# Weights of 40 columns instead of 64 in the state increments of an mLSTM and mixture kernel

## The chip, the cores and the metric

The kernel runs on one core of a Trainium2 chip. The metric is the device time of one execution in microseconds. Three runs of the kernel before took 291.7, 292.54 and 294.46 us; the median is 292.54 us.

## The reference

The first half is an mLSTM attention over 4 batches, 8 heads, 768 steps and a head size of 40. Per step it keeps a matrix state, a vector state and a running maximum of the gates:

```python
m_new = np.maximum(f_gate[:, :, t] + m, i_gate[:, :, t])
f_stab = np.exp(f_gate[:, :, t] + m - m_new)
i_stab = np.exp(i_gate[:, :, t] - m_new)
C = f_stab[:, :, None, None] * C + i_stab[:, :, None, None] * np.einsum('bhd,bhe->bhde', vt, kt)
n = f_stab[:, :, None] * n + i_stab[:, :, None] * kt
y[:, :, t] = o * (C q) / max(|n q|, 1)
```

The second half takes the 320 values per step and runs four experts of causal softmax attention (width 64). Each step's two experts are chosen and weighted by a small gate, and their outputs are projected and summed.

## The kernel before, in words

**Chunks.** The recurrence is worked in chunks of 128 steps, 6 per batch, 24 in all, and each chunk has two subchunks of 64. Inside a chunk the contribution of earlier steps is a masked product (`p1_intra`). What comes from before a subchunk is the state: a table per head of 40 rows (the key's dimensions) by 41 columns (40 value columns and one of ones, which carries the vector state). `p1_inc` forms the state's increment of each subchunk, `sums` adds the masked part and the carried part, and `p1_state` divides by the denominator and applies the output gate.

**Who takes which path.** Chunks 0 to 3 (`NARROW = 4`) go through `inc_narrow`, with weights of 128 rows and 40 columns, and aren't touched. The other 20 go through `p1_inc` (line 1078). Sixteen of them compute both subchunks; the last chunk of each batch computes one.

**The layout.** Even and odd heads lie in the two halves of the partitions for `ks` (the keys times their decay) and `nat` (values and keys). Per head `ks` has `T` = 64 columns; the 40 data columns are rewritten for each chunk by GpSimd, and columns 40 to 63 are zeroed once at the start (line 1551). One increment matmul takes 64 rows of `ks` as weights and 41 columns of `nat` as the moving side, and writes a 64-row half of a bank, so four of them fit on the array side by side. With `wide` (true for every chunk, line 1086), all 64 columns are the weights, so that rows 40 to 63 of the result come out as zeros.

**The evacuation.** Two tiles `pdc` hold the increments. For each subchunk GpSimd multiplies the old state by its decay (`cd`, 112 rows), and VectorE adds the increment to it and writes a tile `sts`. The rows taken are 0 to 111 (`GR` = 64 + 48). The product that uses the state (`carried`, line 1124) reads rows 0 to 39 and 64 to 103, called `heads`.

**The order.** Every engine's instructions are first recorded, and then a planner (`plan`, line 361) puts them in order with prices of its own. It looks up to twelve groups ahead on TensorE where it models a stall of over 350 ns, gives copies to one of two engines by their due times, and times the transfers of SyncE by due times too. The price of a matmul is in `matmul_time` (line 340); for 32-bit weights it is

```python
t = n * 4 / 2.27 + 3
t = max(t, 1.7 * lhs.free_size())
```

with `n` the moving columns and `lhs.free_size()` the weight columns. Due times add these prices up. All instructions are issued from one helper, so the profile gives them all line 618, and tiles tell them apart: `one` is the ring of eight banks of PSUM.

Of the kernel before, what the change touches and what calls it, by code (L numbers as in the profile page):

```python
# [14 lines left out]
B, H, S, D = 4, 8, 768, 40  # L15
# [3 lines left out]
NCH = S // P  # L19
HALF = S // 2  # L20
D1 = D + 1
T = P // 2
RP = 48
GR = T + RP
# [611 lines left out]
def mlstm_moe_kernel(ctx, tc, kq, nat, ig, fg, wqkv, wo, const, out):  # L636
# [9 lines left out]
    def buf(tag, shape, dtype=F32):  # L646
        return View(Buf(rings[tag], shape, dtype))
# [17 lines left out]
    def one(name):  # L665
        tape.cut()
        return buf("one", [P, 512])

    rows = slice(0, T), slice(T, P)
    heads = slice(0, D), slice(T, T + D)  # L670
# [49 lines left out]
    def first(b, j):  # L720
        return b == 0 and j < 3
# [4 lines left out]
    def narrow(b, j):  # L726

        return b * NCH + j < NARROW
# [349 lines left out]
    def p1_inc(b, j):  # L1078
        if narrow(b, j):
            return inc_narrow(b, j)  # L1080
        nm = f"{b}_{j}"
        nt, qc, dm, ks = p1st.pop((b, j, "c"))
        n0 = (b * NCH + j) * 2
        sprev = state[b] if j else None
        sin = [sprev]
        wide = b * NCH + j < 24
        subs = range(2 if j < NCH - 1 else 1)
        pdc = [one(f"pdc_{nm}_{a}") for a in range(2)]
        tape.cut(True)
        for sub in subs:  # L1090
            for g in range(2):
                for z in range(2):
                    for r, p in zip(rows, pdc):
                        nc.tensor.matmul(
                            p[(rows if wide else heads)[z], (2 * sub + g) * D1 : (2 * sub + g + 1) * D1],
                            ks[r, sub, 2 * z + g, 0 : T if wide else D],
                            nt[r, (sub * 4 + 2 * z + g) * D1 : (sub * 4 + 2 * z + g + 1) * D1],
                            start=True,
                            stop=True,
                        )  # L1100
        tape.cut()
        for sub in subs:
            cn = sts[(n0 + sub + 1) % len(sts)][:, : 4 * D1].rearrange("p (g d) -> p g d", g=4)
            if sprev:
                cd = buf("cd", [GR, 4, D1], F32)
                (tape.either if first(b, j) else nc.gpsimd.tensor_tensor)(
                    cd,
                    sprev,
                    dec[:, :, b, 2 * j + sub : 2 * j + sub + 1].to_broadcast([GR, 4, D1]),
                    op=ALU.mult,  # L1110
                )
            for a in range(2):
                x = pdc[a][:, 2 * sub * D1 : 2 * (sub + 1) * D1].rearrange("p (g d) -> p g d", g=2)
                for r in (slice(0, GR),) if wide else heads:
                    if sprev:
                        nc.vector.tensor_tensor(cn[r, a::2, :], x[r], cd[r, a::2, :], op=ALU.add)
                    else:
                        nc.vector.tensor_copy(cn[r, a::2, :], x[r])
            sprev = cn
            sin.append(cn)  # L1120
        state[b] = sprev
        p1st[(b, j, "i")] = (nt, qc, dm, sin)
# [451 lines left out]
    spread(0, 1)  # L1574
    p1_prep(0, 1)
    p1_inc(0, 0)
    p1_intra(0, 1)
    p1_state(0, 0)
    spread(0, 2)
    p1_prep(0, 2)  # L1580
    p1_inc(0, 1)
    p1_intra(0, 2)
    p1_state(0, 1)
    p1_out(0, 0)
    p1_inc(0, 2)
    p1_state(0, 2)
    p1_out(0, 1)
# [110 lines left out]
    for f in LAST.split():  # L1698
        g = dict(f=flip, r=factors, s=score, m=mix, p=project, q=h["queries"], k=h["keys"], v=h["values"], g=h["gate"])
# [65 lines left out]
```

## Time and profile before

| | |
|---|---|
| median of 3 runs | 292.54 us (291.7 to 294.46) |
| profiled execution, span | 291.4 us (the page lists no time of its own beside the span) |
| TensorE matmuls | 279.5 us busy, 96% |
| TensorE weight loads | 242.2 us, 83% |
| VectorE | 220.7 us, 76% |
| ScalarE | 213.8 us, 73% |
| GpSimd | 166.5 us, 57% |
| mean granted clock of TensorE | 0.993 |

A busy time is the sum of the stretches in which at least one instruction of the engine runs. Matmuls overlap, on up to four tiles of the array, and their ends are modelled, so a busy TensorE isn't one at its peak. Weight loads have a row of their own and run beside the matmuls.

### The profile page before, as it was taken

What the parts mean: (1) busy time and instruction counts of PE and PEld (TensorE: products, weight loads), DVE (VectorE), ACT (ScalarE), POOL (GpSimd) and SP (SyncE); (2) the same over time, 40 slices, a digit from 0 to 9 for tenths busy, and PEclk for the clock granted to TensorE, in tenths of its full rate; (3) what the DMA queues carried; (4) which work ended last, traced back from release to release, by engine and by line L of the source; (5) the groups of instructions that cost most, each with busy time, mean ns of one, the idle gap of its engine ahead of it and who ended that gap; (6) DMA issues with size and microseconds to landing.
All of it is one profiled execution on the core that took longest, in us unless ns stands there. A gap on an engine that the chain in (4) does not pass through costs nothing.

```text
span 291.4 us, 12993 instructions
## 1 busy us (share of the span) xinstructions
PE 279.5 (96%) x5128; PEld 242.2 (83%) x5128; DVE 220.7 (76%) x852; ACT 213.8 (73%) x714; POOL 166.5 (57%) x284
## 2 busy tenths in 40 slices
PE   8988999869999999999999999999999999999994
PEld 3876898759889978799889978798989976987884
DVE  7679387847896897657886888577878895588983
ACT  8983459829895887657895887567876895597971
POOL 3678298858889556958587628955870341014000
PEclk9999999979999999999999999999999999999999
DMA  7989769983566455645453537625401000100101
GB/s 217 293 262 282 188 178 236 251 188 110 130 194 184 116 157 167 172 124 169 137 173 112 170 100 200 196 95 146 133 6 71 2 0 2 71 3 0 70 26 45
DMA packets 31580, 39.18 MB, mean 134 GB/s; under 512 B 2784, under 2 KB 25280, under 8 KB 31520
## 3 DMA queue, kind: packets, MB, share of 16 engines
q1 hardware_dynamic: 31472, 38.26, 45.9%
q8 instruction: 40, 0.66, 0.9%
q14 instruction: 20, 0.16, 0.2%
q10 hardware_dynamic: 48, 0.10, 0.1%
HBM read 34.22 MB, written 4.13 MB: 132 GB/s over the span
## 4 chain that ended last, share of the span: by engine, by line
PE 74%; DVE 8%; ACT 5%; issue 4%; DMA 4%; POOL 3%; SPq 1%; DVEq 0%; ACTq 0%; POOLq 0%
PE one L618 74%; DMA nat<-in_nat 4%; ACT dm L618 2%; DVE A L618 2%; POOL qs L618 1%; SPq L618 1%; DVE one L618 1%; DVE sts L618 1%; ACT A L618 1%; POOL yl L618 1%; ACT AT L618 1%; DVE dm L618 0%; DVE facb L618 0%; POOL xt L618 0%; DVE xt L618 0%
## 5 line engine op out<-in xcount | busy, mean ns | idle before, releaser
L618 ACT ACTIVATE A<-A,nmx 128x128 f32<-128x128 f32 (+5 forms) x96 | 64.0, 671 | 3.7 <-DVE nmx L618 3.5
L618 DVE CUSTOM_DVE_ANT_0 A<-one,maskw 128x384 f32<-128x384 f32 (+4 forms) x96 | 45.0, 495 | 0.4
L618 ACT ACTIVATE AT<-one 128x256 f32<-128x256 f32 (+3 forms) x96 | 35.5, 428 | 6.3 <-PE one L618 6.1
L618 PE MATMUL one<-AT,V 128*64 128x384 f32 (+2 forms) x360 | 39.8, 370 | 0.0
L618 PE MATMUL one<-xl,WH 128*128 128x384 f32 x96 | 33.2, 346 | 2.3 <-issue 2.3
L618 PE MATMUL one<-xh,WH 128*128 128x384 f32 x96 | 34.7, 361 | 0.5 <-DVE xt L618 0.5
L618 PEld LDWEIGHTS one<-AT,V 128*64 128x64 f32 x360 | 22.5, 137 | 14.9 <-issue 11.6
L618 POOL TENSOR_TENSOR qs<-kqs,eqs 112x512 f32<-112x512 f32 x20 | 26.2, 1311 | 10.8 <-PE one L618 10.5
L618 PE MATMUL one<-cst,A 64*128 64x64 f32 x672 | 31.6, 226 | 0.0
L618 PEld LDWEIGHTS one<-cst,A 64*128 64x128 f32 x672 | 27.5, 138 | 2.9 <-issue 0.6
L618 POOL TENSOR_TENSOR dm<-dm,cst 128x512 f32<-128x512 f32 x20 | 25.7, 1286 | 6.3 <-DMA dm<-gd 5.0
L618 PE MATMUL one<-KH,QH 64*128 64x384 f32 (+4 forms) x128 | 27.2, 375 | 0.0
L618 POOL TENSOR_TENSOR ks<-nat,dm 128x320 f32<-128x320 f32 x24 | 17.8, 743 | 14.5 <-ACT dm L618 6.9
L618 PE MATMUL one<-KL,QH 64*128 64x384 f32 (+4 forms) x128 | 23.9, 319 | 0.0
L618 PE MATMUL one<-KH,QL 64*128 64x384 f32 (+4 forms) x128 | 23.8, 319 | 0.0
L618 DVE COPY AT<-one 128x384 f32<-128x384 f32 (+3 forms) x48 | 21.0, 456 | 2.5 <-PE one L618 2.2
L618 PEld LDWEIGHTS one<-xh,WH 128*128 128x128 f32 x96 | 18.5, 193 | 4.6 <-issue 3.4
L618 ACT ACTIVATE xh<-one 128x192 fp32r<-128x192 f32 (+1 forms) x45 | 13.0, 335 | 12.3 <-PE one L618 12.2
L618 PE MATMUL one<-xh,WL 128*128 128x384 f32 x64 | 22.0, 343 | 0.0
L618 PE MATMUL one<-WH,xh 128*128 128x260 f32 x72 | 21.5, 301 | 0.0
L618 DVE TENSOR_TENSOR dm<-one,dm 128x256 f32<-128x256 f32 (+1 forms) x44 | 18.7, 440 | 3.3 <-POOL ks L618 3.1
L618 DVE CUSTOM_DVE_ANT_0 A<-one,maskw,nmx 128x320 f32<-128x320 f32 (+1 forms) x32 | 18.5, 579 | 2.8 <-DVE nmx L618 1.0
(143 smaller groups left out, 812.9 us busy)
## 6 DMA issues: line engine op xcount, KB each, us to landing
kqs<-in_kq SPq DMA_DIRECT2D x24, 448.0 KB, 5.6
nat<-in_nat SPq DMA_DIRECT2D x20, 484.0 KB, 5.7
dm<-gd SPq DMA_DIRECT2D x40, 128.0 KB, 3.7
eqs<-ge SPq DMA_DIRECT2D x40, 96.0 KB, 5.3
out<-ob SPq DMA_DIRECT2D x24, 160.0 KB, 1.9
nat<-in_nat SPq DMA_DIRECT2D x4, 320.0 KB, 6.4
A<-in_wqkv SPq DMA_DIRECT2D x3, 386.0 KB, 6.8
nat<-in_nat SPq DMA_DIRECT2D x8, 82.0 KB, 6.3
```

The lines of the kernel that those rows point to most:

```text
L618: f(*[fix(x) for x in op.a], **{k: fix(v) for k, v in op.k.items()})
```

## The change

The increments of the 20 chunks load 40 columns of `ks` as weights and write rows 0 to 39 and 64 to 103 of the bank. The evacuation takes rows 0 to 103 in one instruction. Rows 40 to 63 are then whatever the bank held.

```diff
-        wide = b * NCH + j < 24
...
-                            p[(rows if wide else heads)[z], (2 * sub + g) * D1 : (2 * sub + g + 1) * D1],
-                            ks[r, sub, 2 * z + g, 0 : T if wide else D],
+                            p[heads[z], (2 * sub + g) * D1 : (2 * sub + g + 1) * D1],
+                            ks[r, sub, 2 * z + g, 0:D],
                             nt[r, (sub * 4 + 2 * z + g) * D1 : (sub * 4 + 2 * z + g + 1) * D1],
...
-                for r in (slice(0, GR),) if wide else heads:
+                for r in (slice(0, T + D),):
```

## Rows read from the trace of the kernel before

**Rows 1.** The page: engines' busy times, slices of the span, and the instruction queue.

```profile
PE 279.5 (96%) x5128; PEld 242.2 (83%) x5128; DVE 220.7 (76%) x852; ACT 213.8 (73%) x714; POOL 166.5 (57%) x284
...
PEclk9999999979999999999999999999999999999999
DMA  7989769983566455645453537625401000100101
...
q8 instruction: 40, 0.66, 0.9%
```

**Rows 2.** Stretches: length, busy time and count per engine, granted clock, transfer share, GB/s.

```profile
45.90:59.00 13.10, 11.87 (x368) 10.49 (x369) 11.63 (x57) 11.38 (x52) 11.43 (x15) 1.00 0.99 239
59.00:61.40 2.40, 0.10 (x1) 0.00 (x0) 1.81 (x8) 0.35 (x2) 2.24 (x5) 1.00 1.12 224
61.40:66.00 4.60, 4.56 (x27) 4.21 (x27) 0.56 (x1) 1.38 (x3) 1.52 (x5) 0.63 0.54 145
66.00:114.00 48.00, 47.98 (x1036) 42.69 (x1036) 39.35 (x160) 39.55 (x134) 35.36 (x56) 1.00 0.51 143
114.00:226.00 112.00, 111.54 (x2294) 98.76 (x2290) 85.58 (x344) 82.67 (x280) 74.59 (x122) 1.00 0.46 138
```

**Rows 3.** Waits of TensorE: total us, times, longest us.

```profile
PE one L618 <- issue: 2.3, 1, 2.3
PE one L618 <- DVE sts L618: 1.6, 2, 0.9
```

**Rows 4.** Weight loads by form: rows x columns, count, busy us, mean ns.

```profile
L618 PEld LDWEIGHTS one<-nat,ks 64*64 64x64 f32 x576 | 11.6, 134 | 0.6 <-issue 0.2 <-POOL ks L618 0.2
...
L618 PEld LDWEIGHTS one<-nat,ks 128*40 128x40 f32 x64 | 2.5, 115 | 1.7 <-POOL ks L618 1.7
```

**Rows 5.** Timeline of increments: start us, us from first start to last end.

```profile
13.54 0.74 PE L618 MATMUL one<-nat,ks 128*40 128x82 f32 x16
...
131.44 0.63 PE L618 MATMUL one<-nat,ks 64*64 64x41 f32 x32
...
131.38 0.56 PEld L618 LDWEIGHTS one<-nat,ks 64*64 64x64 f32 x32
```

**Rows 6.** The increments' matmuls by form.

```profile
L618 PE MATMUL one<-nat,ks 128*40 128x82 f32 x64 | 3.0, 235 | 1.2 <-POOL ks L618 1.2
```

**Rows 7.** One short stretch, increments alone: busy us and count of matmuls, of loads, of GpSimd.

```profile
131.44:131.53 0.09, 0.09 (x9) 0.09 (x12) 0.00 (x0) 1.00 0.00 0
```

**Rows 8.** Stretches, loads of the increments alone: length, busy us and count.

```profile
43.00:44.50 1.50, 0.56 (x32) 1.00 1.11 242
...
66.00:226.00 160.00, 9.37 (x464) 1.00 0.48 140
```

**Rows 9.** VectorE sums by form: the state's evacuation, and another sum.

```profile
L618 DVE TENSOR_TENSOR sts<-one,cd 112x82 f32<-112x82 f32 x66 | 12.9, 230 | 5.3 <-POOL cd L618 4.0 <-PE one L618 0.9
...
L618 DVE TENSOR_TENSOR one<-one,pc 64x82 f32<-64x82 f32 x6 | 1.3, 258 | 0.6 <-ACT pc L618 0.6
```

**Rows 10.** Timeline of TensorE around the pause at 59 us.

```profile
61.44 0.33 PE L618 MATMUL one<-xl,WH 128*128 128x384 f32 x1 [2.34 <-issue]
...
61.96 0.51 PE L618 MATMUL one<-xl,WH 128*128 128x384 f32 x1
...
65.15 0.44 PE L618 MATMUL one<-xl,WH 128*128 128x384 f32 x1
...
69.35 0.34 PE L618 MATMUL one<-xl,WH 128*128 128x384 f32 x1
69.53 0.34 PE L618 MATMUL one<-xh,WH 128*128 128x384 f32 x1
```

## The prediction

> **What bounds the kernel now.** I read the page's busy times first, then a table of stretches, then the waits of TensorE. The page shows TensorE busy in nearly every slice and every other engine well below it; the transfers are full only at the start [rows 1]. The stretches say where this holds [rows 2]: from 66 us to 226 us TensorE is busy 159.5 of 160 us (47.98 and 111.54), with VectorE at 0.76 to 0.82, ScalarE at 0.74 to 0.82 and GpSimd at 0.67 to 0.74. Before that, from 45.9 to 59, TensorE is idle 1.2 us and the transfer engines are 0.99 busy; from 59 to 61.4 it stands nearly still. The waits agree [rows 3]: one pause of 2.3 us that waits for no instruction, and a few waits under 1 us. So after 66 us a shorter piece of TensorE work should come through to the end; before 61.4 us it should mostly turn into waiting.
>
> **The weight loads.** A 32-bit matmul of the code stands in the trace as two loads and two matmuls, so the 576 loads of 64 x 64 are the 288 matmuls that the change touches [rows 4]. Does the load set their pace? In an undisturbed group, 32 loads take 0.56 us from the first start to the last end [rows 5]. Less one load of 0.134 us, that is 0.43 us over 31 steps, 13.7 ns each; four array tiles take turns, so each tile is loaded anew every 55 ns, one round. The matmul side would allow less: 16 matmuls of 82 columns on two tiles take 0.74 us in the opening stage [rows 5], less one of 0.235 [rows 6] that is 33.7 ns a step and 67 ns a round, or 34 ns for 41 columns. The load therefore sets the round. Its row falls from 134 to 115 ns when it has 40 columns instead of 64 [rows 4], 19 ns less, which leaves 36 ns by weights.
>
> A third limit is how fast TensorE starts instructions. The group's first matmul starts at 131.44 [rows 5], and from there to 131.53 nine of them have begun [rows 7]: 10 ns apart, 40 ns for a round of four. This is the fastest that the trace shows for this form, and it is above both 36 and 34, so I take 40 ns. The saving is 15 ns a round. Its bounds are 0 (the start rate under load is no better than now) and 55 - 34 = 21 ns.
>
> [...]
>
> **How many rounds count.** Of the 576 loads 464 lie between 66 and 226 us [rows 8], where TensorE has no idle time: 116 rounds, 116 x 15 = 1.7 us (0 to 2.4). The other 112 loads, 28 rounds and 0.4 us, lie from 43 to 58 us, the first of their four groups ahead of 44.5 us [rows 8]; TensorE waits there for transfers and for the pause at 59 us, so I put them at 0 and keep 0.4 us for the range.
>
> **The evacuation.** The same VectorE instructions run with the same free size, on 104 partitions instead of 112. A sum of 82 columns takes 230 ns on 112 partitions, and a like one takes 258 ns on 64 [rows 9]: the time does not follow the partitions. I take 0; 8 fewer partitions reach no row that is read later. Rows 40 to 63 now carry what an earlier user left in the bank, but the carried product takes only rows 0 to 39 and 64 to 103. No instruction is added, and the GpSimd product that decays the state still has its shape, so no queue grows and no new wait stands ahead of anything.
>
> **The written order.** The planner prices one of these matmuls at max(41 x 4 / 2.27 + 3, 1.7 x columns): 109 ns with 64 and 75 ns with 40. Its TensorE time shrinks by about 4 x 34 = 0.13 us for each full chunk, so engine choices for copies and the order on every queue can change from the fifth chunk on, and due times a little earlier. No row prices a queue that isn't written yet. As the expected value I take 0, since the groups that TensorE runs stay the same and it looks ahead only past modelled stalls of 350 ns; the bounds come from the rivals.
>
> **The sum.** 291.4 us span, less 1.7, is 289.7 us. The page gives no device time of this execution beyond its span; the runs lie 0.3 to 3.1 us above it, their median 1.1 us. On the median: 292.5 - 1.7 = 290.8 us.
>
> **Rivals.**
>
> *Nothing comes through.* The start rate stays at 13.7 ns, or VectorE, ScalarE and GpSimd set the pace as soon as TensorE gives way. For: at 0.74 to 0.82 they are not far off, and a TensorE that is always busy in the table may still hold hidden waits, since ends are modelled. Against: 464 loads sit where no wait of TensorE is listed. It gives 292.5 us. That the array tile is loaded as 64 columns whatever the slice would give the same; the 115 ns row speaks against it, though it comes from full-height loads.
>
> [...]
>
> [...]
>
> *The rewritten order is worse.* The state's evacuation comes up behind a score evacuation on VectorE, and TensorE waits for it. The longest such wait now is 0.9 us and there are two [rows 3]. In one chunk in three of the sixteen in which the state is carried after 66 us that is 5 x 0.9 = 4.5 us: 295.3 us. Against: VectorE has a fifth to a quarter of its time free [rows 2].
>
> **The numbers.** Forecast (a saving of 0 to 2.4 us, mostly near 1.7): 0.50, and its own range with the spread of the runs is 289.6 to 292.2. Nothing comes through 0.18; a second starvation 0.12; the pause goes 0.12; a worse order 0.08. A change of under 1%, 2.9 us, can't be told from none, so the limits are 289.6 and 295.5. Faster: the pause that goes, 0.12, and 0.13 of the forecast's 0.50, where the saving is near its upper bound and the median falls low: 0.25. Slower: most of the worse order, 0.06, and a third of the second starvation (with nothing gained, or dearer), 0.04, 0.10. The rest, 0.65, is within 1%. The range runs from 288.4, which leaves out most of the pause that goes, to 294.8, which takes in the second starvation.
>
> **What would show it.** Right: loads of 64 x 40 near 115 ns; 32 of them in about 0.43 us (31 x 10 + 115 ns) instead of 0.56; TensorE still without idle time after 66 us and that stretch 1.7 us shorter; VectorE's sums at 230 ns. Wrong: groups still 0.54 us or more from load to load's end (the start rate rules); shorter groups with new idle time after them (another engine rules); a pause without a releaser at another place, or a second drop of the granted clock; or a stretch before 43 us that has changed its length.

## The result, and the profile after

| | before | after |
|---|---|---|
| median of 11 runs | 294.46 us (291.7 to 296.73) | 291.02 us (289.51 to 291.49) |
| span of the profiled execution | 291.4 us | 289.5 us |

The ratio is 0.9898, with a 95% interval of 0.9873 to 0.9923. It leaves out runs that lie over 1.5% above the fastest of their kernel, which are two of the kernel before. The medians are 3.4 us apart.

The spans are only 1.9 us apart, and that can be reconciled. Where a span and a time of the same execution are both known, the time is 1.8 us longer (289.5 and 291.28 after; 292.2 and 294.0 in a second profile of the kernel before). The execution profiled before was therefore one of about 293.2 us, 1.3 us better than its median; the one after was 0.3 us worse than its own. 1.9 + 1.3 + 0.3 is 3.5.

The page after, the lines that answer to [rows 1]:

```profile
PE 278.5 (96%) x5128; PEld 241.2 (83%) x5128; DVE 219.9 (76%) x851; ACT 212.8 (74%) x712; POOL 167.9 (58%) x287
...
PEclk9999999959999999999999999999999999999999
```

VectorE has one instruction fewer, ScalarE two fewer and GpSimd three more, though the change adds and removes none: the planner has given copies and products to other engines. The order itself is another too.

The increments' loads and VectorE's sum by form (count, busy us, mean ns), which answer to [rows 4, 9]:

```profile
L618 PEld LDWEIGHTS one<-nat,ks 64*40 64x40 f32 x576 | 9.5, 117 | 0.1
...
L618 DVE TENSOR_TENSOR sts<-one,cd 104x82 f32<-104x82 f32 x66 | 13.2, 232 | 5.0 <-POOL cd L618 4.8
```

One group in the timeline (start us, us), as in [rows 5]:

```profile
131.60 0.52 PE L618 MATMUL one<-nat,ks 64*40 64x41 f32 x32
...
131.54 0.45 PEld L618 LDWEIGHTS one<-nat,ks 64*40 64x40 f32 x32
```

A load takes 117 ns instead of 134, and 32 of them 0.45 us instead of 0.56. The sum is at 232 ns, as it was at 230.

Stretches, as in [rows 2] (length, busy us and count per engine, granted clock, transfer share, GB/s):

```profile
45.90:59.00 13.10, 10.25 (x314) 9.06 (x311) 9.20 (x46) 8.73 (x41) 11.04 (x20) 0.92 0.95 229
59.00:61.40 2.40, 2.40 (x81) 2.32 (x80) 1.54 (x6) 2.28 (x12) 0.00 (x0) 0.50 0.60 162
61.40:66.00 4.60, 4.60 (x30) 4.35 (x32) 2.83 (x14) 2.26 (x9) 3.03 (x5) 0.75 0.86 248
66.00:114.00 48.00, 47.88 (x1032) 42.70 (x1028) 40.22 (x163) 40.01 (x134) 35.35 (x55) 1.00 0.51 141
114.00:226.00 112.00, 111.28 (x2308) 98.75 (x2307) 86.64 (x350) 83.26 (x283) 77.40 (x130) 1.00 0.47 139
```

And TensorE around its pause, as in [rows 10]:

```profile
54.18 0.31 PE L618 MATMUL one<-nat,dm 64*64 64x41 f32 x2
57.29 0.51 PE L618 MATMUL one<-nat,dm 64*64 64x41 f32 x9 [2.81 <-issue]
```

The pause is still one pause. It has moved from 59 to 54.5 us, is 0.5 us longer, and the granted clock after it stands at 0.50 for 6.8 us instead of 3.4. After 66 us TensorE is nearly as full as before, 159.2 of 160 us against 159.5.

Where did the 1.9 us between the two spans come from? The increments mark the chunks. To the end of chunk 3's the profile after is 0.9 us later. That isn't work of the new order: TensorE's first product of `cst` and `AT` already starts at 8.31 us instead of 7.43, and up to 21 us both kernels issue everything in the same order. From chunk 3's to chunk 8's it gains 0.2; from chunk 8's to the last chunk's it takes 154.1 us instead of 156.6, a gain of 2.5; the rest, 66.0 us, is the same. So in these two profiles the gain lies after 68 us. The summed lengths of the 20 groups, first to last matmul, fell from 8.64 to 6.88 us.

### The profile page after: what moved, and what is told of

Same layout as the page of the kernel before. It is cut to its first block, busy times and chain, and to the rows that moved or that the text cites. A ratio compares the mean times of both kernels' runs of the same rounds, so it can differ in the third digit from the quotient of the medians.

```text
span 289.5 us, 12979 instructions
## 1 busy us (share of the span) xinstructions
PE 278.5 (96%) x5128; PEld 241.2 (83%) x5128; DVE 219.9 (76%) x851; ACT 212.8 (74%) x712; POOL 167.9 (58%) x287
## 4 chain that ended last, share of the span: by engine, by line
PE 80%; DVE 6%; POOL 4%; ACT 3%; issue 3%; DMA 2%; DVEq 0%; POOLq 0%; ACTq 0%
PE one L618 80%; DMA dm<-gd 2%; ACT A L618 1%; ACT dm L618 1%; DVE A L618 1%; POOL qs L618 1%; DVE sts L618 1%; POOL dm L618 1%; DVE one L618 1%; POOL yl L618 1%; DVE AT L618 1%; POOL AT L618 1%; POOL xt L618 0%; DVE dm L618 0%; DVE xt L618 0%
## 5 line engine op out<-in xcount | busy, mean ns | idle before, releaser
L618 PE MATMUL one<-nat,dm 64*64 64x41 f32 (+1 forms) x704 | 18.5, 234 | 3.3 <-issue 2.8
L618 PEld LDWEIGHTS one<-nat,dm 64*64 64x64 f32 (+1 forms) x704 | 15.4, 138 | 6.5 <-issue 3.6
```

The costliest lines, as they stand in the source:

```text
L618: f(*[fix(x) for x in op.a], **{k: fix(v) for k, v in op.k.items()})
```

## The experiments

"Kernel before" in a row is the one timed beside it on the same chip. Where runs of several kernels are set against each other I use the means over all of them, with a 95% interval from drawing the runs again.

**Loads and order apart.** Two kernels split the change. One takes the narrow loads and keeps the old order:

```diff
-            t = max(t, 1.7 * lhs.free_size())
+            t = max(t, 1.7 * (T if lhs.ap[0][1] == T and lhs.free_size() == D else lhs.free_size()))
```

> The changed kernel, with the planner made to price the narrow increments as 64 columns, so that every queue keeps the order of the kernel before; only the loads are narrow. Theory A (the shorter loads are the whole gain): as fast as the changed kernel, 2 to 3 us under the kernel before, ratio 0.990 to 0.994; the granted clock drops once near 62 us, after a pause of about 2.3 us. Theory B (the rewritten order brings part of it): less than 1.8 us under, ratio 0.994 to 1.000, with the same spread of some 5 us between runs as the kernel before has.

The other keeps 64 columns and takes the new order:

```diff
-            t = max(t, 1.7 * lhs.free_size())
+            t = max(t, 1.7 * (D if n == D1 and out.ap[0][1] == T and self.inc else lhs.free_size()))
```

> The kernel before, with the planner made to price its increments as 40 columns, so that every queue has the order of the changed kernel while the loads stay 64 columns wide. Theory A: no gain, ratio 0.998 to 1.004, or a little slower, since the pause near 55 us costs 0.5 us and 3.4 us of half clock more there. Theory B: 1 to 2 us under the kernel before, and runs that lie within 2 us of each other.

> The changed kernel once more, beside the two others on the same chip. Both theories: ratio 0.987 to 0.993, runs within 2 us of each other, a pause of 2.8 us near 55 us and two low stretches of the clock in a row.

> The kernel before, for a second profile of it. Theory A: the pause near 59 us is there again, within 0.5 us of 2.3 us, with 3.4 us of half clock. Theory B: the pause or the clock after it is another in this execution, by over 1 us, which would make the spread of 5 us between its runs.

| | runs | median us | ratio (95%) |
|---|---|---|---|
| kernel before | 28 | 294.15 (291.07 to 297.69) | |
| narrow loads, old order | 12 | 292.87 | 0.9986 (0.9952 to 1.002) |
| wide loads, new order | 12 | 292.09 | 0.9933 (0.99 to 0.9966) |
| narrow loads, new order | 11 | 290.46 | 0.9898 (0.9862 to 0.9934) |

The narrow loads bring 1.35 us (0.5 to 2.2) in the old order and 1.33 us (0.5 to 2.1) in the new. The new order brings 2.55 us (1.8 to 3.4) with wide loads and 2.5 us (1.7 to 3.5) with narrow. Formed as the ratios of the table are, the two differences against the kernel before are smaller, 0.7 us (-0.2 to 1.4) for the loads in the old order, which can't be told from none, and 1.9 us (1.2 to 2.6) for the order with wide loads; the other two stay. Theory A, that the loads are everything, falls. The wide loads in the new order are 1.2 us (0.4 to 2.0) ahead of the narrow ones in the old, so in the mean the order brings more than the loads.

Part of what the order brings goes with the clock. The mean granted clock differs from run to run, from 0.969 to 1.0. Among the runs at 0.986 to 0.988 the medians are 293.5 us (kernel before, 5 runs), 291.75 (narrow, old order, 5), 292.2 (wide, new order, 6) and 290.3 us (narrow, new order, 4): 1.7 and 1.85 us for the loads, 1.3 and 1.4 for the order. Seven of the twelve runs of narrow loads in the old order lie under that clock, three of the eleven in the new. The runs were sorted after they were known and are few, so this is a hint and not a test: at one clock, loads and order are worth about the same.

My guess that the order narrows the spread of the runs is not borne out: with the old order and narrow loads they lie 4 us apart, with the new order and narrow loads 3.5.

The second profile of the kernel before has its pause at another place, 54.3 us, 2.0 us long and with 6.8 us of low clock. So the pause's place and the clock behind it differ between two executions of the same instructions; these took about 293.2 and 294.0 us. That is a part of the spread between runs, not all of its 5 to 6.6 us.

**What holds the round now.** Two kernels keep the new order and narrow one side further; only the increments' matmuls differ (33 of 41 moving columns; 34 of 40 weight columns as well).

```diff
-                        nc.tensor.matmul(
+                        op = nc.tensor.matmul(
...
+                        o, c = (2 * sub + g) * D1, (sub * 4 + 2 * z + g) * D1
+                        op.a = (
+                            p[z * T : z * T + 34, o : o + 33], ks[r, sub, 2 * z + g, 0:34], nt[r, c : c + 33]
+                        )
```

> The changed kernel, order kept, with 33 moving columns in the increments instead of 41 (the last 8 columns of the state are not updated). It asks what now holds the round of four tiles at 38 ns. Theory A (the moving side, 41 columns): the round falls to 32 to 35 ns. Theory B (weights of 40 columns, or the rate at which TensorE starts instructions, eight in a round): it stays at 37 to 39 ns.

> The changed kernel, order kept, with 34 weight columns and 33 moving columns in the increments (rows and columns of the state left out accordingly). If the weights held the round: 32 to 34 ns, below the run with 33 moving columns alone. If the start rate does: 37 to 39 ns in both.

From the start times of the loads of one group, that of chunk 14 at 129 to 132 us, every fourth load (one round of four tiles), the second to the sixth round:

```
kernel before, 64 weight columns, 41 moving:  57 58 58 59 58 ns, mean 58.0
changed kernel, 40 and 41:                    41 35 41 36 36 ns, mean 37.8
40 and 33:                                    35 37 38 38 39 ns, mean 37.4
34 and 33:                                    34 30 37 30 36 ns, mean 33.4
```

The first round of a group stays at 57 to 60 ns in all four, and the last takes 58, 51, 46 and 53 ns; so from the first to the 29th load the changed kernel takes 298 ns instead of 408. In the rounds between, fewer moving columns change nothing; fewer weight columns do. The weights still hold the round, at 0.84 ns a column (20.2 ns for 24 columns), and a round of eight instructions (four loads, four matmuls) comes every 33.4 ns in the last row, so the start rate didn't.

**The pause.** Both orders, with the loads of two inputs for chunks 5 to 8 cut, `kqs` from 448 to 112 KB and `nat` from 484 to 80 KB (a sixth, where the expectations say a quarter):

```diff
-        nc.sync.dma_start(t[:, :NNAT], nat[b, j])
+        load = nc.sync.dma_start(t[:, :NNAT], nat[b, j])
+        if 5 <= b * NCH + j <= 8:
+            load.a = t[:, 0:160], nat[b, j, :, 0:160]
```

and the same for `kqs`.

> The kernel before with its order kept, but the loads of kqs and nat for chunks 5 to 8 carry only their first quarter, so those chunks compute with stale data. Theory A (the pause near 55 to 59 us is TensorE waiting for its own instructions behind full transfer queues): the pause falls below 0.5 us, the clock stays at its upper level there, the time falls by 3 to 5 us against the kernel before, and the runs lie within 2.5 us of each other. Theory B (the pause is a matter of the written order, not of traffic): pause and half clock stay, the gain is under 1.5 us, the spread stays at 4 us or more.

> The changed kernel with the same loads cut to a quarter for chunks 5 to 8 (stale data there). Theory A: the pause near 55 us and both low stretches of the clock go, 4 to 6 us under the changed kernel; the lead over the old order with the same cut is what the narrow loads and the order after 66 us bring, 2 to 3 us. Theory B: under 1.5 us from the changed kernel.

The old order took 290.47 us (six runs) against 293.8 for the kernel before beside it: 3.0 us less in the mean (1.8 to 4.2). The new order took 286.18 us (six runs): 3.5 us less in the mean than the changed kernel (1.9 to 4.8), which wasn't timed beside it. It leads the old order with the same loads by 4.3 us (2.5 to 6.0), more than the 2 to 3 us that I had expected. The first two rows are the stretches 45.9 to 59 and 59 to 61.4 us of the old order, then those of the new, and then the old order's pause alone:

```profile
45.90:59.00 13.10, 11.66 (x368) 10.36 (x369) 12.60 (x61) 11.44 (x53) 12.39 (x17) 1.00 0.67 170
59.00:61.40 2.40, 1.42 (x9) 1.42 (x9) 0.77 (x4) 0.17 (x1) 1.25 (x4) 1.00 0.98 281
```

```profile
45.90:59.00 13.10, 13.04 (x437) 11.70 (x437) 12.05 (x57) 12.46 (x58) 11.75 (x21) 1.00 0.55 148
59.00:61.40 2.40, 2.40 (x24) 2.15 (x24) 2.23 (x11) 1.91 (x8) 2.04 (x4) 1.00 0.90 258
```

```profile
58.06:59.98 1.92, 0.00 (x1) 0.00 (x0) 1.71 (x8) 0.25 (x2) 1.92 (x4) 1.00 1.07 310
```

In the new order the pause is gone; TensorE is busy 13.04 of 13.10 us and the clock stays up. In the old order a pause of 1.9 us remains at 58.1 us, but the clock stays up behind it (1.00 from 61.4 to 66 us). The transfers are 0.67 busy in the mean of the 13.1 us, yet 1.07 in the pause itself: at that place the smaller loads left them as full as before, so theory A wasn't put to the test there. The early stage is held by the transfers, and their cost is 3 us and more; what the two runs show of the pause agrees with theory A, though not the forecast that it would fall below 0.5 us.

A short pause doesn't need full transfers. With the new order up to chunk 7 (tried further down) TensorE stands for 0.82 us with the transfers at 0.13:

```profile
66.78:67.61 0.83, 0.01 (x3) 0.01 (x2) 0.12 (x1) 0.83 (x5) 0.83 (x1) 0.99 0.13 41
```

What ends it? The trace has the packets of the instruction queue. The transfer queues of the changed kernel between 54.33 and 55.62 us (packets, MB, share of 16 engines):

```profile
q8 instruction: 1, 0.02, 6.2%
```

This one packet of 16 KB begins at 54.34 us, just before TensorE stops at 54.48, and has landed at 55.62; its next matmul begins at 57.29, 1.67 us later. In the profile of the kernel before one lands at 59.91 us and TensorE goes on at 61.44, 1.53 us later; in the old order with less traffic it is 1.56 us. Over all the profiles, the eleven pauses of 0.8 us and more that the profile puts down to "issue" end 1.26 to 1.87 us after such a landing. While the packet moves, the transfers are at 0.95 or more in the seven of 1.9 us and more, and at 0.30 in the one of 0.82 us above. In some others the profile names VectorE's score maximum as the releaser of a pause of 0.9 to 1.4 us near 55 us, with a packet 1.5 to 1.6 us ahead as well; there two causes can't be told apart.

The last of this set takes instructions away, with the traffic as it was (a quarter of the small matmuls of chunks 5 to 8):

```diff
+                        if 5 <= b * NCH + j <= 8 and g:
+                            tape.skip.add(op)
...
+                    if 5 <= b * NCH + j <= 8 and c in (1, 2):
+                        tape.skip.add(op)
```

> The changed kernel, order and transfers kept, without a quarter of TensorE's small matmuls in chunks 5 to 8 (half of the intra scores' groups and half of the masked sums): 256 fewer TensorE instructions between about 46 and 75 us. Theory A (the pause is TensorE running out of fetched instructions): the pause of 2.2 to 2.8 us near 55 us shrinks below 1.2 us or goes. Theory B (it is the transfers alone): a pause of 2 us or more stays, since the traffic is the same.

```profile
57.65 0.34 PE L620 MATMUL one<-kqs 40*64 40x64 f32 x5 [0.81 <-issue]
...
65.69 0.32 PE L620 MATMUL one<-sts,qs 40*64 40x41 f32 x5 [1.28 <-issue]
```

```profile
q8 instruction: 39, 0.64, 1.0%
```

One run took 287.92 us. With 256 instructions of TensorE fewer the queue has 39 packets instead of 40, so I take the packets to carry TensorE's code. The pause has become shorter ones, 0.81 and 1.28 us here, each resumed 1.65 to 1.70 us after a packet (the helper has moved to line 620). With a third, short one they make 2.3 us, as much as the one pause of 2.3 us in the second profile of the changed kernel, but the clock stayed up at 55 to 65 us (the run's mean granted clock is 0.994). It fits a TensorE that waits for its instructions, without settling it: the longest is 1.28 us where I had said under 1.2, none is 2 us long as theory B has it, and the total is no less. Nearly all of the 40 packets of a run pass without such a pause: the first profile of either kernel has one wait on "issue" in which TensorE stands, of 2.3 and of 2.8 us. If the fetch is the cause, the pauses of 1.9 to 3.2 us are the exceptions.

**Where the order's gain lies.** Narrow loads, with the new price for chunks 4 to 7 alone, or from chunk 8 on alone:

```diff
+        tape.old = b * NCH + j >= 8
```

(and `< 8` in the second; `old` prices the increments with 64 columns)

> Narrow loads throughout; the planner prices them as 40 columns for chunks 4 to 7 and as 64 columns from chunk 8 on, so that the order of the changed kernel holds up to about 75 us and another follows. Theory A (the order's gain of 2 us lies before 66 us, where the pauses are): as fast as the changed kernel within 0.7 us, ratio 0.986 to 0.990. Theory B (it lies after 66 us, in score groups whose two tiles fall out of step): 1.5 to 2.5 us slower than the changed kernel, ratio 0.993 to 0.997.

> Narrow loads throughout; the planner prices them as 64 columns for chunks 4 to 7 and as 40 columns from chunk 8 on: the order of the kernel before up to about 75 us, another after it. Theory A: 1.5 to 2 us slower than the changed kernel, ratio 0.992 to 0.997. Theory B: as fast as the changed kernel within 0.7 us, ratio 0.986 to 0.990. If the gain is half here and half there, both of these two lie near 0.991.

| | runs | median us | ratio (95%) |
|---|---|---|---|
| new order up to chunk 7 | 12 | 292.05 | 0.9926 (0.9894 to 0.9957) |
| new order from chunk 8 | 6 | 290.28 | 0.9866 (0.9827 to 0.9906) |

The late part alone is as fast as the changed kernel (290.46; 0.2 us more in the mean, -0.6 to 1.1); the early part alone is 0.8 us under the old order with narrow loads (292.87), which these intervals do not part from nothing. The two were not timed beside those they are set against; the kernel before took 294.17 us beside the one pair and 294.15 beside the other. This speaks for theory B, that the gain is after 66 us. The order of either half is not a copy of one of the two known ones past its seam, so the halves need not add up.

The profiles show only part of it there. From chunk 8's increments to the last, the old order with narrow loads takes 155.8 us and the changed kernel 154.1; with wide loads it is 156.6 and 157.0 us in the two profiles of the kernel before and 155.9 in the new order. That is 1.7 and 0.7 to 1.1 us of an order's gain of 2.5; where the rest lies isn't shown, and the clock ahead of 66 us is the likeliest place.

Two places make most of the 1.7 us: the step from chunk 15's increments to chunk 16's is 0.73 us shorter and that from 21's to 22's is 0.69, together 1.4 us.

At the first place VectorE forms a product from SBUF. The old order with narrow loads, VectorE and then GpSimd:

```profile
141.24 1.05 DVE L618 TENSOR_TENSOR xt<-xt,den 128x320 f32<-128x320 f32 x1
```

```profile
141.21 0.74 POOL L618 TENSOR_TENSOR ks<-nat,dm 128x320 f32<-128x320 f32 x1
```

In the changed kernel:

```profile
142.37 0.49 DVE L618 TENSOR_TENSOR xt<-xt,den 128x320 f32<-128x320 f32 x1
```

```profile
142.57 0.89 POOL L618 TENSOR_TENSOR ks<-nat,dm 128x320 f32<-128x320 f32 x1
```

Begun 0.03 us after GpSimd's product, VectorE's takes 1.05 us; begun 0.2 us ahead of it, 0.49. TensorE's six transposes of `xt` then take 0.57 us from first to last instead of 0.40, and the chunk's scores begin 0.3 us later behind them; the rest of the 0.73 us was not followed. It is no accident of one pair of profiles: in all but that of the last experiment VectorE makes this product beside GpSimd's. It takes 0.96 to 1.07 us in the five where it starts second and 0.49 or 0.50 in the eight where it starts first, and the step from chunk 15's increments to 16's takes 7.5 to 8.1 us in the five and 7.1 to 7.4 in the eight. In both pairs of rows the product that starts second is the slower one: VectorE's at 1.05 us instead of 0.49, GpSimd's at 0.89 instead of 0.74. It ends 0.34 and 0.60 us behind the earlier one. What holds it back is not shown.

At the second place the old order holds a bank. TensorE in the old order, with narrow loads, and in the changed kernel:

```profile
209.90 0.30 PE L618 MATMUL one<-kqs 40*64 40x64 f32 x2
210.42 0.63 PE L618 MATMUL one<-kqs 40*64 40x64 f32 x27 [0.22 <-DVE nmx L618]
```

```profile
210.23 0.71 PE L618 MATMUL one<-kqs 40*64 40x64 f32 x31
```

The third score matmul waits for VectorE to finish a score evacuation, which began late, at 209.81 (0.53 us idle before it, waiting for ScalarE):

```profile
209.81 0.55 DVE L618 CUSTOM_DVE_ANT_0 A<-one,maskw,nmx 128x320 f32<-128x320 f32 x1 [0.53 <-ACT A L618]
```

The same wait stands in the kernel before, at 211.96 us. In the changed kernel the same evacuation begins after 0.17 us and the scores run through.

**A price nearer the chip.** If the planner knew the chip's 58 ns a round, would its order be better?

```diff
-            t = max(t, 1.7 * lhs.free_size())
+            t = max(t, 1.83 * lhs.free_size())
```

> The changed kernel with the planner's price of a weight column at 1.83 ns instead of 1.7, so that matmuls with 64 weight columns are priced at 117 ns, which is two rounds of 58 ns as the kernel before shows them. Theory A (a price nearer the chip gives a better order): 0.5 to 2 us under the changed kernel, ratio 0.982 to 0.987. Theory B (a re-planned order is as likely worse as better, within some 2 us): anywhere from 0.983 to 0.998.

296.72 us (12 runs), ratio 1.0077 (1.0051 to 1.0103): 2 to 3 us slower than the kernel before and 6 us slower than the changed kernel. Theory A falls, and theory B's range, up to 0.998, was too narrow as well. Its profile has a pause of 3.2 us at 53 us and 10.2 us of low clock behind it. The loss lies there: chunk 8's increments end 3.3 us later than in the changed kernel, and from there to the last chunk's it takes 154.7 us against 154.1. One re-planned order gained some 2.5 us and another lost as much, and no price that I know tells which.

## Why the prediction was right or wrong

- **The sum and the level.** 290.8 us was forecast and 291.02 measured, but the agreement is partly luck: the three runs shown gave 292.54 for the kernel before, and 28 gave 294.15. The move was 3.4 us and not 1.7.
- **The loads: right in mechanism, a little large.** 1.7 us (0 to 2.4) was forecast, 1.33 and 1.35 us were measured (0.7 in the old order, formed as the ratios are). The sum of 116 rounds at 15 ns holds for the group: from its first load to the next load of other work it is 0.62 us before and 0.50 after, the 0.12 us forecast. That is partly luck too, since the rounds in the middle save 20 ns each and the first and the last little.
- **The limit of the round: wrong.** I took 40 ns from the start rate, and 36 ns for the weights. The weights hold it, at 37.8 ns; eight starts fit into 33 ns. The 55 ns that I worked out for the kernel before is 58: a merged row's length hides that the first four loads start in a burst, within 20 ns.
- **The written order: the step that failed.** "As the expected value I take 0, since the groups that TensorE runs stay the same". It brought 2.5 us in the mean, more than the loads; at one clock, 1.3 or 1.4. A warning stood in the rows, VectorE and GpSimd at 0.67 to 0.82 beside a full TensorE; the two places where it told were found only after the runs. No row gave the sign or the size, and that is a reason for a term of some 2 us on both sides of the range and not for 0. The rival "worse order" had 4.5 us in the wrong direction, and a better order had no rival beyond the pause that goes away.
- **The evacuation: right.** 232 ns against 230.
- **Nothing comes through: wrong**, both parts came through.
- **A second starvation, or none: neither.** There is one pause still, longer and at another place. It moves between executions of the same kernel, from 59 to 54.3 us. No run shows what one pause more or fewer is worth, on which the two chances of 0.12 and the ends of the range rest. The runs showed pauses of 2.0 to 2.8 us in the two profiles of each kernel, and with less traffic 3.0 us less in the old order, where a pause of 1.9 us stays without the low clock, and 3.5 us less in the new, where it goes.
- **The signs of being wrong.** Two that it named came: a pause at another place, and a stretch before 43 us of another length. Neither speaks against the sum, as both also differ where the order of the work is the same.

## What to carry to other kernels

When a planner or a scheduler reads an instruction's size as its price, a change of shape is two changes: time the new shape in the old order and the old shape in the new order before crediting either. Here the shape gave 1.3 us and the order 2.5 in the mean over the runs. For packed small matmuls on four tiles like these, narrowing the weights shortened the round by 0.84 ns a column from 64 to 40 and by 0.67 from 40 to 34. It should end where the moving side takes longer, 34 ns for 41 columns by the prediction's estimate; no run here reached that limit.

## What the runs showed of the hardware that I had not expected

- TensorE's pause follows a 16 KB packet of its instruction queue and ends 1.26 to 1.87 us after it has landed. The pauses of 1.9 us and more all have the transfers at 0.95 or above while the packet moves; one of 0.82 us has them at 0.30. Whether the packet is the cause, and whether it is asked for too late or is held up, is open.
- To chunk 3's increments four profiles with the old early order take 36.1 us and a fifth 36.6; those with the new one take 36.5 to 38.3. The difference is there by 9.5 us (0.4 to 1.6 us), where both orders issue the same work in the same order, and stays as it is up to 42 us; the two longest, 38.2 and 38.3 us, add 0.6 us with 3.4 us of low clock at 24 us. So the order of the work doesn't make it, and what does was not tried.
- A VectorE product over SBUF doubled from 0.49 to 1.05 us by starting 0.03 us behind a GpSimd product instead of 0.2 us ahead.
